# Block-sparse attention with a gated MLP on one core: batch 0's PSUM evictions, a dealing table and two early copies

## The chip, the core and the metric

The kernel runs on one core of a Trainium2 chip. Five engines have queues of their own: PE (TensorE, the matmuls), DVE (VectorE), ACT (ScalarE), POOL (GpSimd) and SP (SyncE, which issues most transfers here). The metric is the device time of one launch in microseconds, the median over runs. Lower is better.

## The reference

Attention over 4 batches, 8 heads, 768 positions and 64 dimensions, with a block mask (blocks of 32: neighbours, first and last blocks, and three sampled blocks per row); its output, heads side by side, goes into a gated MLP that mixes along the sequence.

```python
scores = scale * np.matmul(q, k.transpose(0, 1, 3, 2))
scores = np.where(mask, scores, -1000000000.0)
scores = scores - np.max(scores, axis=-1, keepdims=True)
attn = np.exp(scores)
attn = attn / (np.sum(attn, axis=-1, keepdims=True) + 1e-09)
x = np.matmul(attn, v)            # to (batch, seq, heads*dim)
...
h = np.maximum(x @ w_in, 0.0)
u, v = (h[..., :d_ff // 2].copy(), h[..., d_ff // 2:].copy())
mu = np.mean(v, axis=-1, keepdims=True)
var = np.mean((v - mu) ** 2, axis=-1, keepdims=True)
v_n = (v - mu) / np.sqrt(var + 1e-06)
v_s = np.einsum('ts,bsd->btd', w_spatial, v_n) + b_spatial[None, :, None]
gated = u * v_s
return (gated @ w_out).astype(np.float32)
```

## The kernel before

**Pairs and slots.** Two heads of a batch make a pair: 16 pairs, 4 to a batch. The order of all work is written out by hand as a list of slots (the loop at L837). Slots 0 to 35 do the four pairs of batch 0 in thirds of the queries, as its inputs arrive. From slot 36 on, a head takes six slots, one for each 128 keys, and a pair twelve; pair p starts at slot 36 + 12(p - 4) (`slot_of`, L805). Slots 36 to 83 hold batch 1's scores, 84 to 131 batch 2's, 132 to 179 batch 3's.

**What a slot does.** In order: two score matmuls into a PSUM tile "sc" (L455) and one exponential of it on ACT (L459); six matmuls of probabilities times values (L506) of the head seven slots back; whatever `when` put into the slot; some steps of the queue of gMLP matmuls (`run_queue`, L707); and what was put off to its end. PSUM has two "sc" tiles, so a slot's scores need the exponential of two slots before to be over, two "av" tiles for the values' product, and two banks "moeA" and "moeB" that the gMLP products (and some transposes) take in turn. A head's last slot divides by the sums on DVE: a reciprocal (L470) and a multiplication (L471), "the scaling" below.

**The gMLP of a batch** runs beside the attention of the next one, as products of 128 tokens by 512, each a list of steps of one matmul of 128x512 (`product`, L573; all have line L580). v0 to v5 and u0 to u5 (four steps each) are the two halves of x times `w_in`; s0 to s5 (six steps) are the spatial mix of the normalized v; o0 to o5 (four steps) the product with `w_out`. The last step of a product calls `done`, which records its eviction from the bank:
- v: maximum with 0 on DVE (L610; ACT in the last batch), and its statistics; POOL makes the reciprocal deviation; the norm (L634) comes some steps later on DVE, and all that are left just before s0 (L695);
- u: maximum with 0, on DVE for u0 to u3 of batch 0 (L640), on ACT for the others (L642). The helper `ts` records at L186;
- s: plus bias, times u, on DVE (L648); after every second one a transposing DMA from SP (L658) makes the operand of o;
- o: a copy into a result tile `osb`, on ACT for even and on DVE for odd numbers (L675; the copies record at L221 and L218), followed by its DMA to memory from SP (L677).

**How the steps are dealt.** `STEPS` (L771) fixes the number of steps for slots 20 to 41. At slot 42 the last 16 input steps of batch 0, its 36 spatial and 24 output steps, 76 in all, are dealt over 50 slots by a running credit (L712 to L719), which gives 1 or 2 a slot. At slots 92 and 140 the gMLP of batches 1 and 2 starts: 108 steps over 48 slots.

**The score operands.** q and k of pairs 4 to 15 are loaded, cast on POOL (L137), transposed by a DMA from SP (`tr_dma`, L411, tile `tt`, 20 slots before the pair's start), and copied to `kq` by DVE, one head at a time: `split(p, 0)` five slots before the pair starts (L814) and `split(p, 1)` three before (L815), 64x1536 each, recorded at L218. `tt` has two buffers. Pair 9 starts at slot 96 and pair 13 at slot 144.

**In-order queues.** Each engine does its instructions in the order in which they were recorded, slot by slot: an instruction that waits holds up all that were recorded behind it on its engine.

Of the kernel before, what the change touches and what calls it, by code (L numbers as in the profile page):

```python
# [26 lines left out]
def kernel(  # L27
# [37 lines left out]
    TW = TC * 128  # L65
    S0 = NT * NG * 3
    FILL, FILL2, FILL3 = 24, 4, 4
    U_DVE = (0, 1, 2, 3)

    const = ctx.enter_context(tc.tile_pool(name="const", bufs=1))  # L70
    work = ctx.enter_context(tc.tile_pool(name="work", bufs=1))
# [112 lines left out]
    def ts(out, in0, s1, o0, s2=None, o1=None):  # L184
        kw = {} if o1 is None else {"op1": o1}
        nc.vector.tensor_scalar(out=out, in0=in0, scalar1=s1, scalar2=s2, op0=o0, **kw)  # L186
# [334 lines left out]
    def xtr_pe(p, xn, c0, n, ps=None):  # L521
        if ps is None:
            ps = bank()
        for c in range(n):
            tr(ps, c, pair_of(xn, c))
        dve_copy(xt_tile(p)[:, c0 * 128:(c0 + n) * 128], ps[:, 0:n * 128])
# [46 lines left out]
    def product(n, lhs, rhs, last, done, w=512):  # L573
        ref = {}
        out = []
        for i in range(n):
            def run(i=i):
                if i == 0:
                    ref["ps"] = moe_ps(last)
                nc.tensor.matmul(out=ref["ps"][:, 0:w], lhsT=lhs(i), rhs=rhs(i),  # L580
                                 start=(i == 0), stop=(i == n - 1))
                if i == n - 1:
                    done(ref["ps"][:, 0:w])
            out.append(run)
        return out
# [4 lines left out]
    class Moe:  # L590
# [45 lines left out]

        def u_product(self, tcc):
            def done(ps):
                if self.b == 0 and tcc in U_DVE:
                    ts(self.un[:, tcc, :], ps, 0.0, ALU.max)  # L640
                else:
                    nc.scalar.activation(out=self.un[:, tcc, :], in_=ps, func=AF.Relu)  # L642
            return product(NDM, lambda g: self.xt(g, tcc), lambda g: w_in_t[:, g, 0:DH],
                           self.last, done)
# [19 lines left out]
        def o_product(self, tcc):  # L664
            steps = []
            osb = {}
            parts = 2 if self.last and tcc == NCH - 1 else 1
            w = DM // parts
            for i in range(parts):
                cs = slice(i * w, (i + 1) * w)  # L670

                def done(ps, i=i, cs=cs):
                    if i == 0:
                        osb["t"] = work.tile([128, DM], FP32, tag="osb", bufs=6, name="osb")
                    on_act = (tcc + i) % 2 == 0  # L675
                    (act_copy if on_act else dve_copy)(osb["t"][:, cs], ps)
                    (nc.scalar if i or (self.last and tcc == 0) else nc.sync).dma_start(  # L677
                        out=out[self.b].rearrange("(p c) d -> c p d", c=NCH)[tcc][:, cs],
                        in_=osb["t"][:, cs])
                steps += product(NDH, lambda d: self.gt[:, tcc, d, :],  # L680
                                 lambda d, cs=cs: w_out_t[:, d, cs], self.last, done, w)
            return steps
# [20 lines left out]
    def deal(steps, slots):  # L703
        queue.extend(steps)
        pace["slots"], pace["credit"] = slots, 0.0

    def run_queue(n=None):  # L707
        if n is not None:
            for _ in range(n):
                queue.popleft()()  # L710
            return
        if not queue or pace["slots"] <= 0:  # L712
            return
        pace["credit"] += (len(queue) - pace["credit"]) / pace["slots"]
        pace["slots"] -= 1
        n = int(pace["credit"] + 0.5)
        for _ in range(min(n, len(queue))):
            queue.popleft()()
            pace["credit"] -= 1  # L719
# [5 lines left out]
    def when(slot, *fns):  # L725
        at.setdefault(slot, []).extend(fns)

    def c(f, *a, **kw):
        return lambda: f(*a, **kw)
# [29 lines left out]
    def close_first():  # L759
        first["steps"].popleft()()  # L760
        if moe_tags[0] not in held:
# [7 lines left out]
    when(20, close_first)  # L769
    when(29, lambda: deal(moe[0].in_steps("v2 v3 u2 u3", TC), 14))  # L770
    STEPS = {20: 1, 21: 2, 22: 1, 23: 1, 24: 2, 25: 1, 26: 1, 27: 2, 28: 1, 29: 1, 30: 1, 31: 1, 32: 2, 33: 1, 34: 1, 35: 1, 36: 1, 37: 0, 38: 1, 39: 2, 40: 2, 41: 2}  # L771
    when(42, lambda: deal(moe[0].in_steps("v4 v5 u4 u5", TC) + moe[0].rest_steps(),
                          S0 + 8 + 48 - 42))
    for b in (1, 2):
# [30 lines left out]
    def slot_of(p):  # L805
        return S0 + 12 * (p - NG)

    for p in range(NG, NP):
        g = slot_of(p)
        when({4: 13, 5: 22, 6: 31}.get(p, g - 34), c(load, p, "k"), c(load, p, "q"), c(load, p, "v"))  # L810
        when({4: 18, 5: 26, 6: 38}.get(p, g - 25),
             c(cast, p, "k", PL), c(cast, p, "q", PL), c(cast, p, "v", PL))
        when({4: 20, 5: 30}.get(p, g - 20), c(tr_dma, p))
        when(g - 5, c(split, p, 0))  # L814
        when(g - 3, c(split, p, 1))  # L815
        if p == NP - 1:
            when(g + 20, last_x)
        elif p % NG == NG - 1:
            when(g + 20, lambda p=p: xtr_pe(p, xn_ref.pop(("p", p)), 0, NCH))
        else:  # L820
            when(g + 20, c(xtr_dma, p))
# [15 lines left out]
    for s in range(NS + LAG + 2):  # L837
# [11 lines left out]
        for f in early:  # L849
            f()  # L850
        run_queue(STEPS.get(s))
        for f in late.get(s, []):
# [34 lines left out]
```

## Time and profile before

| | |
|---|---|
| Median of 3 runs | 212.64 us (212.44 to 212.85) |
| The profiled execution | 212.95 us |
| Its span, first to last instruction | 211.1 us (211.06) |
| Granted TensorE clock | 0.999 |
| PE busy | 205.2 us, 2141 matmuls |
| ACT busy | 169.8 us, 225 instructions |
| DVE busy | 129.3 us, 290 instructions |
| POOL busy | 69.8 us |
| Exponential of a slot from 36 on (L459) | 144, median 0.811 us |
| u evictions of batch 0 on DVE, 128x512 from PSUM (L186) | 4, 0.692 us each |
| u evictions on ACT out of moeA and moeB (L642) | 14, median 0.592 us |
| o evictions on ACT out of moeA and moeB (L221) | 9, median 0.592 us |
| Copy of a score operand to `kq` from `tt` (L218) | 24, median 0.555 us |
| Transposing DMA into `tt`, issue to landing | median 6.6 us, 3.8 to 8.5 |

A matmul's busy time in the profile includes its way through the array, and matmuls overlap, so "97% busy" does not say that PE never stands still. The starts say it: matmuls that wait for nothing start at a fixed distance from one another. An exponential starts some 0.69 to 0.71 us after the one before where it waits for nothing, though its own time is 0.81, since instructions of ACT and DVE overlap by their last part.

### The profile page before, as it was taken

To read this page: it belongs to the slowest core of one execution; us is meant where nothing else is said; L and a number is where in the kernel's file an instruction comes from. 1 tells how busy PE (TensorE), PEld (TensorE's weight loads), DVE (VectorE), ACT (ScalarE), POOL (GpSimd) and SP (SyncE) were. 2 spreads that over 40 slices of the span, in tenths; PEclk is the share of its full clock that TensorE was granted. 3 is DMA by queue.
4 is the path that set the end of the run, shared out by engine and by line. 5 is a ranking of instruction groups with operands and counts; after the bars stand their busy time and mean duration, and the time that the engine had idled before them with its cause. 6 is when DMAs were issued, how large, how long until landed. Compare 5 with 4: busy or idle time off the path is not lost.

```text
span 211.1 us, 5272 instructions
## 1 busy us (share of the span) xinstructions
PE 205.2 (97%) x2141; PEld 128.7 (61%) x2141; DVE 129.3 (61%) x290; ACT 169.8 (80%) x225; POOL 69.8 (33%) x108
## 2 busy tenths in 40 slices
PE   8998999999999999999999999999999999999993
PEld 6687878765666665665565566565565566544441
DVE  6798584687844534385888445287685433567542
ACT  5798999998999999979999788979989878266021
POOL 6583959756574224042533031040120000003000
PEclk9999999999999999999999999999999999999999
DMA  5999899999999999999991399695100423520276
GB/s 161 347 340 296 248 338 295 302 189 293 254 368 237 271 188 314 219 290 370 131 282 36 60 245 224 205 274 160 37 3 5 80 54 77 208 103 0 40 163 246
DMA packets 64295, 41.97 MB, mean 199 GB/s; under 512 B 45184, under 2 KB 59024, under 8 KB 64272
## 3 DMA queue, kind: packets, MB, share of 16 engines
q1 hardware_dynamic: 63696, 41.06, 76.0%
q10 hardware_dynamic: 576, 0.59, 0.8%
q8 instruction: 16, 0.26, 0.5%
q14 instruction: 7, 0.06, 0.1%
HBM read 24.38 MB, written 6.29 MB: 145 GB/s over the span
## 4 chain that ended last, share of the span: by engine, by line
PE 81%; DMA 10%; ACT 2%; DVE 1%; POOL 1%; SPq 1%; issue 1%; ACTq 0%
PE ps_moe L580 30%; PE ps L455 22%; PE ps_av L506 12%; PE ps_t L580 8%; DMA tt<-nat 4%; DMA w_f<-in_moe_w_in_dram 4%; PE ps_sc L580 4%; DMA ws_f<-in_moe_w_spatial_dram 3%; PE ps L442 2%; PE wps L180 1%; ACT a_all L459 1%; DVE kq L218 1%; PE ps_av L488 1%; POOL w_in_t L234 1%; PE ps L289 1%
## 5 line engine op out<-in xcount | busy, mean ns | idle before, releaser
L459 ACT ACTIVATE a_all<-ps 128x768 bf16<-128x768 f32 x144 | 113.8, 813 | 14.0 <-PE ps L455 7.0
L455 PE MATMUL ps<-kq 88*128 88x384 bf16 x288 | 70.4, 325 | 0.2
L506 PEld LDWEIGHTS <-a_all 128*128 128x128 bf16 x864 | 45.2, 97 | 20.0
L506 PE MATMUL ps_av<-vv,a_all 128*128 128x65 bf16 x864 | 49.8, 193 | 0.0
L455 PEld LDWEIGHTS <-kq 88*128 88x128 bf16 x288 | 28.0, 97 | 31.2 <-issue 1.1
L580 PE MATMUL ps_moe<-w_in_t,xt 128*128 128x512 bf16 x144 | 43.8, 378 | 0.2 <-POOL w_in_t L234 0.2
L447 ACT ACTIVATE a_all<-ps 128x1024 bf16<-128x1024 f32 x36 | 34.9, 1025 | 3.1 <-PE ps L442 2.5
L580 PE MATMUL ps_moe<-vn,w_spt 128*128 128x512 bf16 x108 | 32.7, 378 | 0.0
L137 POOL CAST nat<-st_k 128x768 bf16<-128x768 f32 (+2 forms) x17 | 13.6, 803 | 44.3 <-DMA st_k<-in_k_dram 43.6
L442 PE MATMUL ps<-kq 88*128 88x256 bf16 (+1 forms) x140 | 23.0, 287 | 0.2 <-ACT a_all L447 0.2
L470 DVE RECIPROCAL rc<-ps_av 128x6 f32<-128x6 f32 (+1 forms) x36 | 6.6, 184 | 26.7 <-PE ps_av L506 25.9
L648 DVE SCALAR_TENSOR_TENSOR un<-ps_moe,b_col,un 128x512 bf16<-128x512 f32 x18 | 13.5, 750 | 15.3 <-PE ps_moe L580 14.7
L617 POOL TENSOR_SCALAR std<-mv 128x3 f32<-128x3 f32 (+1 forms) x9 | 2.2, 240 | 59.9 <-DVE mv L614 43.9
L580 PE MATMUL ps_moe<-w_out_t,gt 128*128 128x512 bf16 x72 | 21.5, 378 | 0.0
L580 PEld LDWEIGHTS <-xt 128*128 128x128 bf16 x192 | 15.5, 98 | 7.3 <-DVE xt L218 0.2
L471 DVE TENSOR_TENSOR xn<-ps_av,rc 128x384 bf16<-128x384 f32 (+1 forms) x36 | 18.5, 513 | 1.2
L613 DVE BATCH_NORM_STATS2 stats<-vn 128x6 f32<-128x512 bf16 x24 | 16.5, 687 | 1.4 <-ACT vn L608 0.9
L137 POOL CAST nat<-st_q 128x768 bf16<-128x768 f32 (+2 forms) x21 | 14.5, 695 | 7.8 <-DMA st_q<-in_q_dram 7.6
L137 POOL CAST vv<-st_v 128x768 bf16<-128x768 f32 x16 | 13.6, 848 | 7.9 <-DMA st_v<-in_v_dram 7.7
L442 PEld LDWEIGHTS <-kq 88*128 88x128 bf16 x140 | 13.0, 100 | 4.5 <-issue 0.8
L218 DVE COPY kq<-tt 64x1536 bf16<-64x1536 bf16 x24 | 14.3, 595 | 2.3 <-DMA tt<-nat 2.1
L580 PEld LDWEIGHTS <-w_spt 128*128 128x128 bf16 x144 | 11.4, 98 | 5.2
(81 smaller groups left out, 205.8 us busy)
## 6 DMA issues: line engine op xcount, KB each, us to landing
st_v<-in_v_dram SPq DMA_DIRECT2D x16, 384.0 KB, 6.0
st_k<-in_k_dram SPq DMA_DIRECT2D x15, 384.0 KB, 4.0
out_dram<-osb SPq DMA_DIRECT2D x22, 256.0 KB, 3.5
st_q<-in_q_dram SPq DMA_DIRECT2D x12, 384.0 KB, 5.4
ws_f<-in_moe_w_spatial_dram SPq DMA_DIRECT2D x6, 384.0 KB, 9.0
w_f<-in_moe_w_in_dram SPq DMA_DIRECT2D x8, 256.0 KB, 7.9
w_f<-in_moe_w_out_dram SPq DMA_DIRECT2D x4, 256.0 KB, 4.0
st_q<-in_q_dram SPq DMA_DIRECT2D x6, 128.0 KB, 5.4
```

The source lines that it names most:

```text
L137: eng.tensor_copy(out=dst, in_=src)
L218: nc.vector.tensor_copy(out=o, in_=i)
L442: nc.tensor.matmul(out=ps[:, at:at + n * TW], lhsT=kq[:, h, ci * 128:(ci + 1) * 128], rhs=kq[:, h, qcols(t0, n)], start=True, stop=True)
L447: nc.scalar.activation(out=out, in_=ps, func=AF.Exp, scale=0.125)
L455: nc.tensor.matmul(out=ps[:, hf * 512:hf * 512 + HALF], lhsT=kq[:, j % H, ci * 128:(ci + 1) * 128], rhs=kq[:, j % H, S + hf * HALF:S + (hf ...
L459: nc.scalar.activation(out=a_ref["h", j][:, ci, :].rearrange("p (b c) -> p b c", b=2), in_=ps.rearrange("p (b c) -> p b c", b=2)[:, :, 0:H ...
L470: nc.vector.reciprocal(out=rc[:, 0:n], in_=ps[:, :, D:VA])
L471: nc.vector.tensor_tensor(out=out, in0=ps[:, :, 0:D], in1=rc[:, 0:n].to_broadcast([128, n, D]), op=ALU.mult)
L506: nc.tensor.matmul(out=av_ref[j][:, qc, 0:VA], lhsT=a_ref["h", j][:, ci, qc * 128:(qc + 1) * 128], rhs=vv[p % NVV][:, h, ci, 0:VA], start= ...
L580: nc.tensor.matmul(out=ref["ps"][:, 0:w], lhsT=lhs(i), rhs=rhs(i), start=(i == 0), stop=(i == n - 1))
L613: nc.vector.bn_stats(out=stats, in_=self.vn[:, tcc, :])
L648: nc.vector.scalar_tensor_tensor(out=self.un[:, tcc, :], in0=ps, scalar=b_col[:, tcc:tcc + 1], in1=self.un[:, tcc, :], op0=ALU.add, op1=AL ...
```

## The change

Three things. (1) In batch 0, u4 and u5 and then o0, o2 and o4 are evicted by DVE too, so all of its u and o products are. (2) `STEPS` gets entries for slots 42 to 91, so the credit rule no longer decides there; the steps themselves and their order stay. (3) For pairs 9 and 13 the first of the two copies to `kq` is recorded seven slots before the pair's start (slots 89 and 137) instead of five (91 and 139). The numbers of instructions on PE, POOL and SP and their order there stay, but for the place of three gMLP matmuls among PE's; DVE gets five instructions more and ACT five fewer.

```diff
@@ -65,7 +65,6 @@
     FILL, FILL2, FILL3 = 24, 4, 4
-    U_DVE = (0, 1, 2, 3)
@@ -636,7 +635,7 @@
         def u_product(self, tcc):
             def done(ps):
-                if self.b == 0 and tcc in U_DVE:
+                if self.b == 0:
                     ts(self.un[:, tcc, :], ps, 0.0, ALU.max)
                 else:
                     nc.scalar.activation(out=self.un[:, tcc, :], in_=ps, func=AF.Relu)
@@ -672,7 +671,7 @@
-                    on_act = (tcc + i) % 2 == 0
+                    on_act = (tcc + i) % 2 == 0 and (self.last or self.b > 0)
                     (act_copy if on_act else dve_copy)(osb["t"][:, cs], ps)
@@ -769,6 +768,8 @@
     STEPS = {20: 1, 21: 2, 22: 1, 23: 1, 24: 2, 25: 1, 26: 1, 27: 2, 28: 1, 29: 1, 30: 1, 31: 1, 32: 2, 33: 1, 34: 1, 35: 1, 36: 1, 37: 0, 38: 1, 39: 2, 40: 2, 41: 2}
+    STEPS.update({s: 2 if (s % 2 == 0) == (s < 67) else 1 for s in range(42, 92)})
+    STEPS.update({43: 2, 46: 1})
     when(42, lambda: deal(moe[0].in_steps("v4 v5 u4 u5", TC) + moe[0].rest_steps(),
                           S0 + 8 + 48 - 42))
@@ -811,7 +812,7 @@
-        when(g - 5, c(split, p, 0))
+        when(g - (7 if p in (9, 13) else 5), c(split, p, 0))
         when(g - 3, c(split, p, 1))
```

## The prediction

> **What bounds the kernel now.** I read the page first: the busy shares and the chain that ended last.
>
> ```profile
> PE 205.2 (97%) x2141; PEld 128.7 (61%) x2141; DVE 129.3 (61%) x290; ACT 169.8 (80%) x225; POOL 69.8 (33%) x108
> ...
> PE 81%; DMA 10%; ACT 2%; DVE 1%; POOL 1%; SPq 1%; issue 1%; ACTq 0%
> ```
>
> TensorE is the bound, and the other engines hold 2% and 1% of the chain. A change that leaves TensorE's instructions as they are, as this one does, can only win back the moments in which TensorE stands still. Second I read the chain in order of time from 47 to 58 us (start, duration, what) to price a slot.
>
> ```profile
> 48.05 0.31 issue
> 48.37 0.82 ACT a_all L459
> 49.19 0.04 issue
> 49.23 0.48 PE ps L455 x2
> ...
> 51.99 0.33 PE ps L455 x2
> ...
> 52.72 0.33 PE ps L455 x2
> ...
> 53.66 0.33 PE ps L455 x2
> ```
>
> A slot begins with its two score matmuls (L455). From 51.99 to 52.72 is a slot with one gMLP matmul, 0.73; from 52.72 to 53.66 one with two, 0.94. So a slot is 0.51 for scores and attention (0.33 + 0.18) and 0.215 for each gMLP matmul. Laying this grid over the score starts from slot 36 (42.65 us) to the last slot leaves five holes after 43 us: 0.27 in slot 43 (48.23 to 49.23 with one gMLP matmul, 1.00 against 0.73), 0.18 in slot 51, 0.24 in slot 80, and 0.15 and 0.10 where batches 1 and 2 begin (slots 92 and 140). All else is on the grid within 0.01. The change can reach about 0.9 us at most.
>
> Third I looked for what made each hole. Slot 43: the first lines above. The exponential of slot 42 starts 0.31 after the last one ended, for no cause that the profile shows ("issue"), and the score bank that slot 44 needs comes free so much later. Slot 51, in TensorE's timeline:
>
> ```profile
> 55.17 0.49 PE L455 MATMUL ps<-kq 88*128 88x384 bf16 x2
> ...
> 56.08 0.48 PE L455 MATMUL ps<-kq 88*128 88x384 bf16 x2
> ...
> 56.80 0.38 PE L580 MATMUL ps_moe<-vn,w_spt 128*128 128x512 bf16 x1
> ```
>
> 0.91 for a slot of 0.73. ScalarE evicts u4 at 54.73, ahead of slot 50's exponential (55.21 to 56.03), which holds the score bank that slot 52 needs. Slot 80 is the same with o0, in ScalarE's timeline:
>
> ```profile
> 79.28 0.59 ACT L221 ACTIVATE osb<-ps_moe 128x512 f32<-128x512 f32 x1
> ```
>
> The scores at 80.62 wait for the exponential behind it. The other three evictions (u5 57.31, o2 83.52, o4 88.53) cost TensorE nothing: the slots around them are on the grid. Slot 92's hole is VectorE's:
>
> ```profile
> 89.65 0.54 DVE L218 COPY kq<-tt 64x1536 bf16<-64x1536 bf16 x1
> 90.16 0.69 DVE L218 COPY osb<-ps_moe 128x512 f32<-128x512 f32 x1
> ```
>
> v0 of batch 1 needs o5's bank and starts at 90.90, that is 0.05 after this eviction ends; six transposes from 90.42 at 0.055 would have let it start at 90.75.
>
> **The table.** The old rule dealt 76 gMLP matmuls over slots 42 to 91 as 2,1,2,1,2,1,1,2,1,2... Written out, the table gives the same count in every slot but two: slot 43 gets 2 instead of 1, slot 46 gets 1 instead of 2. So v4's last matmul and the next two come a slot earlier; 73 of 76 stay. Slot 43 then has 0.94 of work in the 1.00 that it lasts anyway, and slot 46 shrinks from 0.94 to 0.73: **-0.215**. v4's eviction does not move: VectorE runs back to back there (norm 50.26, eviction 51.09), and v5's first matmul waits for u3's eviction, over at 48.36. If the pause at 48.05 does not come, slot 43 grows by what slot 46 shrinks: 0.
>
> **The u evictions.** Two ScalarE instructions of 0.59 to 0.62 go; slot 51 returns to 0.73: **-0.18**. Two VectorE instructions come; the rows for the same shape (u0 to u3) are 0.692 each. They stand behind the attention scaling of 55.40 and ahead of the two norms:
>
> ```profile
> 55.40 0.56 DVE L471 TENSOR_TENSOR xn<-ps_av,rc 128x384 bf16<-128x384 f32 x1
> 56.45 1.24 DVE L186 TENSOR_SCALAR vn<-vn,mv,rstd 128x512 bf16<-128x512 bf16 x2 [0.49 <-POOL rstd L619]
> ```
>
> From 49.46 to 55.96 VectorE has no idle time, and its start there is set by GpSimd (rstd, 48.70 + 0.73), not by TensorE: this run of work does not move with the gain. After such a scaling the next instruction starts 0.475 later (89.18 to 89.65), so u4's eviction runs from 55.88 to 56.57. Its bank is the one that the first spatial product s0 takes. s0 started at 56.805; by the two gains it would be ready at 56.805 - 0.215 - 0.18 = 56.41, and can start at 56.57 + 0.05 = 56.62: **+0.21**, a new wait. u5's eviction follows at 56.6 (its last matmul ends then) to 57.3, the norms to 58.2 or, stretched as the second is now, 58.5; s0's fifth and sixth matmuls need them at 59.0 and 59.7, the attention scaling behind them moves from 58.45 to at most 58.5, and its bank is not asked for before slot 61. Nothing for these.
> By the row the move costs 0.10 more per eviction than on ScalarE (0.692 against 0.59). The Trainium skill speaks against it too: "Perfetto Trace Analysis", section Optimizing Scalar/DVE Operations, gives a fixed cost of about 125 ns for VectorE on PSUM and about 51 ns for ScalarE. By that the move would cost 0.074, and the new wait would come out at an estimated 0.18; the trace agrees in sign and is the dearer.
>
> **The o evictions.** Three of 0.59 leave ScalarE; slot 80 returns to 0.73: **-0.24**. Three VectorE copies of 0.692 (rows of o1, o3, o5) come. o0 goes in at 79.40 behind a scaling and pushes the two score-operand copies to 81.2, wanted at slot 84 (83.2). o2 fills idle time at 83.4; the reciprocal behind it moves from 83.94 to 84.1. o4 ends at 88.9, where the reciprocal waited until 88.95. The banks are asked for 1.9 to 2.2 us after these ends (slots 81, 87, 92). SP, which sends the results in order, is busy with a transpose until 83.5 when o0 is ready and sends o2 at 87.0 and o4 at 93.2 as now. Nothing but the gain.
>
> **The two splits.** Each is one VectorE copy of 0.54, no DMA; its transfer is issued where it was. Pair 9's goes from behind the scaling of 89.18 to before o4's eviction, where VectorE idles from 86.57. o5's eviction then waits for its matmul alone (ends 90.07): 90.10 instead of 90.16, **-0.05**. Pair 13's leaves 137.73, but the eviction behind it (138.40) already starts 0.04 after its matmul (137.99 + 0.38): 0. The copies' sources landed at 85.5 and 129.1 by the semaphore's events, before the new places (86.6, 135.8).
>
> **Sum.** -0.215 - 0.18 + 0.21 - 0.24 - 0.05 = -0.475. From slot 92 on only slot 140 and the last output have holes (0.10 each), both of TensorE's own timing, so the gain should reach the end. The profiled execution took 212.95 (span 211.06 and 1.89 around it), 0.31 above the median of the three runs, 212.64. It would come to 212.48; the median to 212.64 - 0.475 = **212.17**.
>
> **Rivals.**
> *The pause is chance.* The gap at 48.05 is the only one of its kind on ScalarE in the trace, and the profiled execution is the slowest of the four times, by 0.31 against the median. Then the table gives nothing, and s0 would have started at 56.54 before; after, still 56.62: +0.08. With -0.24 and -0.05 the gain is 0.21: 212.43. Against it: every wait of that exponential had long been met, so it may be part of the program's own stream, which is unchanged there.
> *No new wait.* In VectorE's full stretch one norm took 0.91 (50.26) where its neighbour took 0.41, and a copy 1.02 (52.73) where others take 0.55, each while GpSimd cast (50.20, 52.51). If the loads that start those casts land 0.3 earlier or later, the stretch ends 0.5 or 0.95 sooner, and s0 does not wait: -0.685, 211.95. The skill's page "SBUF — State Buffer", Who interferes with whom, says that a VectorE instruction in a two-port mode and GpSimd lock each other out for a whole instruction; these rows agree.
> *The early split blocks VectorE: slower.* In its new place pair 9's copy stands ahead of o4's eviction, the last scaling of batch 0's queue, o5's eviction and v0. Issued at 80.29, its source took 5.2 us; such transposes took 3.8 to 8.5. At 8.5 it lands at 88.8; then copy to 89.35, o4 to 90.0, reciprocal and scaling to 90.7, o5 to 91.4, v0 at 91.45 against 90.43: +1.02, 0.55 slower than before, 213.19. It begins to cost at a landing of 87.3, and has eaten the gain at 88.2. For it: its queue is loaded there; against it: 1.8 us to spare in this trace.
> *It does not do what it says.* The table moves three matmuls, so half of the sum hangs on slots 51 and 80; if other executions have holes elsewhere the time stays: 212.6.
>
> **How the numbers follow.** A difference under 0.2% (0.43 us) can't be told from none. Forecast 0.50, of which 0.33 lies beyond 0.43 and 0.17 within, since 0.475 is so near; pause by chance 0.20 (within); no new wait 0.17 (faster); blocked split 0.08 (slower); no effect 0.05 (within). Faster 0.50, same 0.42, slower 0.08. The range takes the cases from 211.95 to 212.6 with the runs' own spread (0.2 each way): 211.8 to 212.8, leaving out the slower case and the edges.
>
> **What would show it.** Right: score starts 0.73 apart across slots 46, 51 and 80; s0's first matmul 0.05 after a VectorE un eviction that ends near 56.6; v0 of batch 1 at 90.4; batch 1's slots on the same grid. Wrong: a hole of 0.1 or more in slots 76 to 92 behind VectorE, a copy that waits for its transpose near 87 to 89, or a grid that is itself slower.

## The result, and the profile after

| | before | changed |
|---|---|---|
| Median of 15 runs each, side by side | 212.42 us (211.98 to 213.35) | 211.59 us (210.38 to 212.13) |
| Changed to before, 95% interval | | 0.9957 (0.994 to 0.9974) |
| Profiled execution | 212.95 us | 211.57 us |
| Its span | 211.06 us | 209.80 us |
| Start to the scores of slot 37 | 43.60 | 42.76 |
| Scores of slot 37 to scores of slot 179 | 133.94 | 133.33 |
| From there to the last matmul's end | 30.06 | 30.04 |
| Last matmul's end to the span's end | 3.46 | 3.67 |

The changed kernel is faster, by 0.4%, and by the first comparison it lies just below the range forecast. The lower rows part the two spans (43.60 + 133.94 + 30.06 + 3.46 = 211.06) and already say that the 1.26 us between them are of three kinds: 0.84 lies before slot 37, where no instruction was changed; 0.61 lies in the slots that the change reaches; and 0.21 is given back at the very end.

The page of the profile after: the shares of the engines, and the chain that ended last.

```profile
PE 203.2 (97%) x2141; PEld 127.8 (61%) x2141; DVE 134.2 (64%) x295; ACT 167.8 (80%) x220; POOL 69.3 (33%) x108
...
PE 86%; DVE 6%; DMA 4%; ACT 2%; POOL 1%; issue 0%; ACTq 0%; SPq 0%
```

The five instructions have gone from ACT (225 to 220) to DVE (290 to 295), and PE is still the bound. The chain runs through DVE and DMA (6% and 4%) only in the first 42.3 us, and through PE alone from there to the last output. Line numbers of the changed kernel are one lower than those of before: scores L454, exponential L458, gMLP L579.

TensorE's timeline of the changed kernel, in the slots where the prediction put its first two terms and its new wait (start, duration, what):

```profile
47.39 0.49 PE L454 MATMUL ps<-kq 88*128 88x384 bf16 x2
...
47.90 0.59 PE L579 MATMUL ps_moe<-w_in_t,xt 128*128 128x512 bf16 x2
48.38 0.48 PE L454 MATMUL ps<-kq 88*128 88x384 bf16 x2
...
54.11 0.49 PE L454 MATMUL ps<-kq 88*128 88x384 bf16 x2
...
54.84 0.49 PE L454 MATMUL ps<-kq 88*128 88x384 bf16 x2
...
55.56 0.38 PE L579 MATMUL ps_moe<-vn,w_spt 128*128 128x512 bf16 x1
55.78 0.49 PE L454 MATMUL ps<-kq 88*128 88x384 bf16 x2
```

Slot 43 (47.39 to 48.38) holds two gMLP matmuls now, and with the pause in it still lasts 0.99. Slot 51, from 54.11 to 54.84, is 0.73, not the 0.91 of before. Slot 52 (54.84 to 55.78) holds one more u5 matmul and s0's first, and is 0.94, exactly two gMLP matmuls: the wait of 0.21 that the prediction put in front of s0 is not there. VectorE's timeline says why:

```profile
47.74 0.41 DVE L185 TENSOR_SCALAR vn<-vn,mv,rstd 128x512 bf16<-128x512 bf16 x1 [0.22 <-POOL rstd L618]
48.07 0.54 DVE L217 COPY kq<-tt 64x1536 bf16<-64x1536 bf16 x1
48.53 0.91 DVE L185 TENSOR_SCALAR vn<-vn,mv,rstd 128x512 bf16<-128x512 bf16 x1
...
53.67 0.56 DVE L470 TENSOR_TENSOR xn<-ps_av,rc 128x384 bf16<-128x384 f32 x1
54.15 0.68 DVE L185 TENSOR_SCALAR un<-ps_moe 128x512 bf16<-128x512 f32 x1
...
86.95 0.55 DVE L217 COPY kq<-tt 64x1536 bf16<-64x1536 bf16 x1 [1.86 <-DMA tt<-nat]
87.43 0.68 DVE L217 COPY osb<-ps_moe 128x512 f32<-128x512 f32 x1
...
88.72 0.68 DVE L217 COPY osb<-ps_moe 128x512 f32<-128x512 f32 x1
```

u4's eviction (54.15 to 54.83) stands right behind the scaling, 0.48 after its start, as forecast. But the whole stretch began at 47.74, only 0.35 after the scores of slot 43 (47.39); before, it began at 49.46, 1.23 after them (48.23). VectorE is 0.88 earlier against TensorE, and s0's bank is free 0.73 before s0 comes. The stretched norm (0.91) is still there, so the stretch did not become shorter; it was begun earlier. The lines of before on which this rests, of GpSimd and VectorE:

```profile
43.96 0.83 POOL L137 CAST vv<-st_v 128x768 bf16<-128x768 f32 x1 [1.84 <-DMA st_v<-in_v_dram]
45.23 3.07 POOL L552 CAST ws_b<-ws_f 128x768 bf16<-128x768 f32 x2 [0.44 <-DMA w_spt<-ws_b]
...
48.70 0.73 POOL L619 TENSOR_TENSOR rstd<-std,mhalf 128x2 f32<-128x2 f32 x1
49.46 0.41 DVE L186 TENSOR_SCALAR vn<-vn,mv,rstd 128x512 bf16<-128x512 bf16 x1 [1.10 <-POOL rstd L619]
```

The last three lines of the changed kernel's VectorE timeline, from 86.95, are pair 9's early copy and the evictions of o4 and o5. The copy waited for its transpose (idle 1.86, released by the DMA), o4's eviction followed at 87.43 and o5's at 88.72, behind VectorE's own work and not behind its matmul. Slot 92's hole is 0.18 against 0.15 before: what the slower rival described did begin, and cost 0.03.

### The profile page after: what moved, and what is told of

Read it like the earlier page. It is cut to its first block, busy times and chain, and to the rows that moved or that the text cites. A ratio compares the mean times of both kernels' runs of the same rounds, so it can differ in the third digit from the quotient of the medians.

```text
span 209.8 us, 5271 instructions
## 1 busy us (share of the span) xinstructions
PE 203.2 (97%) x2141; PEld 127.8 (61%) x2141; DVE 134.2 (64%) x295; ACT 167.8 (80%) x220; POOL 69.3 (33%) x108
## 4 chain that ended last, share of the span: by engine, by line
PE 86%; DVE 6%; DMA 4%; ACT 2%; POOL 1%; issue 0%; ACTq 0%; SPq 0%
PE ps_moe L579 32%; PE ps L454 22%; PE ps_av L505 13%; PE ps_t L579 8%; DMA w_f<-in_moe_w_in_dram 4%; PE ps_sc L579 4%; PE ps L441 3%; DVE kq L217 2%; PE ps_av L487 2%; ACT a_all L446 1%; DVE vn L185 1%; PE wps L179 1%; PE ps L288 1%; DVE stats L612 1%; DVE xn L470 1%; POOL w_in_t L233 1%
## 5 line engine op out<-in xcount | busy, mean ns | idle before, releaser
L458 ACT ACTIVATE a_all<-ps 128x768 bf16<-128x768 f32 x144 | 114.1, 811 | 15.1 <-PE ps L454 7.4
L454 PE MATMUL ps<-kq 88*128 88x384 bf16 x288 | 70.4, 325 | 0.0
L454 PEld LDWEIGHTS <-kq 88*128 88x128 bf16 x288 | 28.0, 97 | 30.6 <-issue 0.2
L579 PE MATMUL ps_moe<-w_in_t,xt 128*128 128x512 bf16 x144 | 43.8, 378 | 0.6 <-POOL w_in_t L233 0.6
L579 PE MATMUL ps_moe<-vn,w_spt 128*128 128x512 bf16 x108 | 32.7, 377 | 0.0
L441 PE MATMUL ps<-kq 88*128 88x256 bf16 (+1 forms) x140 | 21.7, 275 | 1.0 <-DVE kq L217 0.5
L579 PE MATMUL ps_moe<-w_out_t,gt 128*128 128x512 bf16 x72 | 21.5, 378 | 0.0
L579 PEld LDWEIGHTS <-xt 128*128 128x128 bf16 x192 | 15.5, 98 | 7.3 <-DVE xt L217 0.2
L217 DVE COPY kq<-tt 64x1536 bf16<-64x1536 bf16 x24 | 15.6, 650 | 2.5 <-DMA tt<-nat 2.2
L579 PEld LDWEIGHTS <-w_spt 128*128 128x128 bf16 x144 | 11.4, 98 | 5.2
```

What stands on the lines that cost most here:

```text
L217: nc.vector.tensor_copy(out=o, in_=i)
L441: nc.tensor.matmul(out=ps[:, at:at + n * TW], lhsT=kq[:, h, ci * 128:(ci + 1) * 128], rhs=kq[:, h, qcols(t0, n)], start=True, stop=True)
L454: nc.tensor.matmul(out=ps[:, hf * 512:hf * 512 + HALF], lhsT=kq[:, j % H, ci * 128:(ci + 1) * 128], rhs=kq[:, j % H, S + hf * HALF:S + (hf ...
L458: nc.scalar.activation(out=a_ref["h", j][:, ci, :].rearrange("p (b c) -> p b c", b=2), in_=ps.rearrange("p (b c) -> p b c", b=2)[:, :, 0:H ...
```

## The experiments

All holes below are by the grid of the prediction (0.51 and 0.215 for each gMLP matmul, and 0.33 for the six transposes of slots 92 and 140), in slots 43 to 178; slots 37 to 42 hold other matmuls and are alike within 0.02 in all profiles. "37 to 179" is the time between the scores of these two slots.

| Kernel | 37 to 179, us | holes over 0.1, by slot | first norm behind slot 43's scores | last matmul's end to span's end |
|---|---|---|---|---|
| before | 133.94 | 43: 0.27, 51: 0.18, 80: 0.24, 92: 0.15, 140: 0.10 | 1.23 | 3.46 |
| changed | 133.33 | 92: 0.18, 140: 0.10 | 0.35 | 3.67 |
| e1_table | 134.11 | 51: 0.18, 80: 0.24, 92: 0.16, 140: 0.49 | 0.61 | 3.47 |
| e2_u | 133.80 | 43: 0.27, 80: 0.24, 92: 0.16, 140: 0.14 | 0.05 | 3.49 |
| e3_o | 133.71 | 43: 0.28, 51: 0.18, 92: 0.16, 140: 0.10 | 0.38 | 3.68 |
| e4_split | 133.94 | 43: 0.27, 51: 0.18, 80: 0.24, 92: 0.16, 140: 0.10 | 1.30 | 3.53 |
| a2_again | 133.32 | 92: 0.16, 140: 0.10 | 0.05 | 3.72 |
| a3_again | 133.31 | 92: 0.15, 140: 0.10 | 0.05 | 3.68 |
| a_no_split | 133.32 | 92: 0.16, 140: 0.10 | 0.05 | 3.64 |
| a_before2 | 133.94 | 43: 0.27, 51: 0.18, 80: 0.24, 92: 0.16, 140: 0.10 | 0.05 | 3.45 |
| b_act4 | 133.69 | 51: 0.18, 80: 0.24, 92: 0.16, 140: 0.10 | 0.05 | 3.51 |
| a_late_deal | 132.86 | none | 0.05 | 3.65 |
| a_late_act4 | 132.80 | none | 0.40 | 3.66 |
| a_dve_late2 | 137.04 | 52: 2.09, 54 to 56: 1.64 in all, 92: 0.16, 140: 0.10 | 0.72 | 3.64 |

### One part of the change at a time

**e1_table**: the kernel before with the table alone.

```diff
+    STEPS.update({s: 2 if (s % 2 == 0) == (s < 67) else 1 for s in range(42, 92)})
+    STEPS.update({43: 2, 46: 1})
```

> The kernel before with the table alone. Theory A (each part fills its own hole in TensorE's grid of slots; what lies before slot 36 differs from execution to execution and has nothing to do with the change): slot 43 keeps its length near 1.0 us with two gMLP matmuls in it, slot 46 shrinks from 0.94 to 0.73, the holes of slots 51 and 80 stay, so slots 37 to 178 get 0.2 shorter; time lower by 0.2 (0.1%). Theory B (the parts only pay together, or the gain lies in slots 0 to 35, through where instructions lie in their streams): less than 0.05 between slots 37 and 178, or a slot 36 that starts 0.5 or more before 42.6. If the pause of 0.31 on ScalarE in slot 42 is chance, it is missing here and nothing is gained.

Slot 43 went from a hole of 0.27 to 0.05 with the same pause in it: the second matmul lies where TensorE stood. Against before, 37 to 179 is 0.18 longer, since a hole of 0.39 more opened in slot 140, far behind the table's slots; without it the gain is 0.21. Time 212.26 (12 runs) against 212.61 (35 runs), ratio 0.999 (0.9961 to 1.0019). The new hole is the one that the split of pair 13 is about. VectorE's timeline of this kernel there:

```profile
137.72 1.16 DVE L218 COPY kq<-tt 64x1536 bf16<-64x1536 bf16 x1
138.80 0.67 DVE L218 COPY osb<-ps_moe 128x512 f32<-128x512 f32 x1
```

and TensorE's:

```profile
138.70 0.50 PE L289 MATMUL ps<-ident,xn 128*128 128x128 bf16 x6
139.53 0.59 PE L580 MATMUL ps_moe<-w_in_t,xt 128*128 128x512 bf16 x2 [0.33 <-DVE osb L218]
```

In the old place the copy can take 1.16 and not 0.54: here GpSimd casts beside it (137.64 to 138.47), while in the profile of before that cast was over at 137.69 and the copy began at 137.73. o5's eviction then ends at 139.47, and v0 of batch 2 waits for it until 139.53.

**e2_u**: the u evictions alone.

```diff
-                if self.b == 0 and tcc in U_DVE:
+                if self.b == 0:
```

> The kernel before with u4 and u5 of batch 0 evicted by VectorE, nothing else. Theory A: slot 51's hole (0.18) is gone, s0's first matmul waits for u4's eviction only if VectorE's full stretch (the norm behind the first rstd) starts 1.0 us or more after slot 43's scores, as in the profile of before (1.23); then s0 would start without the table's gain at about the same time as the eviction ends, so 0.1 to 0.18 gained between slots 37 and 178. Theory B: nothing there, gain in slots 0 to 35 or none.

The hole of slot 51 (0.18) went, and nothing came in slot 52. TensorE's timeline shows slots 51 and 52 at 0.72 and 0.95:

```profile
55.09 0.49 PE L455 MATMUL ps<-kq 88*128 88x384 bf16 x2
...
55.81 0.49 PE L455 MATMUL ps<-kq 88*128 88x384 bf16 x2
...
56.54 0.38 PE L580 MATMUL ps_moe<-vn,w_spt 128*128 128x512 bf16 x1
56.76 0.49 PE L455 MATMUL ps<-kq 88*128 88x384 bf16 x2
```

VectorE evicted u4 at 54.45, and s0 came at 56.54. The start of VectorE's stretch was 0.05 behind slot 43's scores. Time 211.93, ratio 0.9986 (0.9956 to 1.0016).

**e3_o**: the o evictions alone.

```diff
-                    on_act = (tcc + i) % 2 == 0
+                    on_act = (tcc + i) % 2 == 0 and (self.last or self.b > 0)
```

> The kernel before with o0, o2 and o4 of batch 0 evicted by VectorE, nothing else. Theory A: slot 80 goes from 0.97 to 0.73, slots 43 and 51 keep their holes, slot 92's hole stays at 0.15 or grows by up to 0.1 since o4's eviction and the copy now both stand ahead of o5's: 0.15 to 0.25 gained between slots 37 and 178, time lower by 0.1%. Theory B: nothing there.

The hole of slot 80 (0.24) went; the slot is 0.73 long:

```profile
78.12 0.49 PE L455 MATMUL ps<-kq 88*128 88x384 bf16 x2
...
78.85 0.49 PE L455 MATMUL ps<-kq 88*128 88x384 bf16 x2
```

The end grew by 0.2, to 3.68. Time 212.07, ratio 0.9994 (0.9966 to 1.0021).

**e4_split**: the two early copies alone.

```diff
-        when(g - 5, c(split, p, 0))
+        when(g - (7 if p in (9, 13) else 5), c(split, p, 0))
```

> The kernel before with the first copies of pairs 9 and 13 two slots sooner, nothing else. Theory A: slot 92's hole shrinks by 0.05 at most where pair 9's transpose has landed by 86.5, and grows where it lands later than 87.3; slot 140 unchanged at 0.10; time the same within 0.1%. Theory B: a gain of 0.2 or more from this part.

Nothing moved: 37 to 179 in 133.94, slot 92's hole 0.157 (0.154 before). Time 212.67, ratio 1.0007 (0.9981 to 1.0033). VectorE's timeline of this kernel ahead of slot 92:

```profile
88.21 0.55 DVE L218 COPY kq<-tt 64x1536 bf16<-64x1536 bf16 x1 [1.58 <-DMA tt<-nat]
89.00 0.20 DVE L470 RECIPROCAL rc<-ps_av 128x6 f32<-128x6 f32 x1 [0.24 <-PE ps_av L506]
...
90.21 0.69 DVE L218 COPY osb<-ps_moe 128x512 f32<-128x512 f32 x1 [0.42 <-PE ps_moe L580]
```

With the copy out of the way, o5's eviction still starts only when its matmul is over ("<-PE ps_moe"), at the same place on TensorE's grid. So TensorE itself set it before too, and the copy ahead of it was not what it waited for. The early copy again waited 1.58 for its transpose, here without cost.

The parts add up: 0.21 + 0.18 + 0.24 = 0.63, less 0.03 in slot 92, gives 0.60, and the changed kernel gained 0.61. None of the four times can be told from the kernel before: every interval holds 1. What each part does is read from the grid.

### Is the new wait real, and what decides it?

**a_before2**: the kernel before, profiled once more, with no edit.

> The kernel before, unchanged, profiled once more. My theory: its holes in slots 43, 51 and 80 come again within 0.02 (0.27, 0.18, 0.24), its time from slot 37 to 179 is 133.94 within 0.05; VectorE's first norm starts anywhere from 0.05 to 1.3 behind slot 43's scores, and the start of slot 36 lies anywhere from 41.1 to 42.9. The rival (the late start of VectorE, 1.23, is a property of the kernel before): 1.2 to 1.3 again.

VectorE's timeline of this run:

```profile
46.97 0.69 DVE L186 TENSOR_SCALAR un<-ps_moe 128x512 bf16<-128x512 f32 x1 [0.47 <-PE ps_moe L580]
47.58 0.53 DVE L186 TENSOR_SCALAR vn<-vn,mv,rstd 128x512 bf16<-128x512 bf16 x1
48.03 0.54 DVE L218 COPY kq<-tt 64x1536 bf16<-64x1536 bf16 x1
48.50 0.40 DVE L186 TENSOR_SCALAR vn<-vn,mv,rstd 128x512 bf16<-128x512 bf16 x1
49.45 0.69 DVE L186 TENSOR_SCALAR vn<-ps_moe 128x512 bf16<-128x512 f32 x1 [0.55 <-PE ps_moe L580]
```

The same kernel as in the prediction, and none of what the prediction read there: the first norm follows u3's eviction at once, 0.05 behind slot 43's scores (47.53), the second takes 0.40, and VectorE then idles 0.55 for TensorE. The holes are the same within 0.01 and so is 37 to 179, 133.94 (one run, 212.73 us). So the holes are a property of the kernel, and the late start of VectorE was one of that execution. GpSimd's timeline of this run says what differed:

```profile
42.29 3.09 POOL L552 CAST ws_b<-ws_f 128x768 bf16<-128x768 f32 x2 [1.81 <-DMA w_spt<-ws_b]
...
45.77 0.73 POOL L619 TENSOR_TENSOR rstd<-std,mhalf 128x2 f32<-128x2 f32 x1
```

In the profile of before GpSimd stood 1.84 for a load of v (`st_v`), until 43.96, and its long cast of `w_spatial` started 3.00 ahead of slot 43's scores. Here it could cast that load at 39.65, the long cast started 5.24 ahead of them, and the reciprocal deviation (`rstd`) was there long before the norm asked for it.

**a_dve_late2**: the changed kernel with VectorE made late by six memsets. They write a tile that nothing reads.

```diff
+    late_t = const.tile([128, 256], FP32, name="late_t")
...
+    when(49, lambda: [nc.vector.memset(late_t, 0.0) for _ in range(6)])
```

> The changed kernel with six memsets of a 128x256 tile (read by nobody) recorded on VectorE in slot 49, inside the stretch in which it has no idle time. My theory (s0 waits by how late VectorE's stretch runs: wait = start of the first norm behind slot 43's scores, plus the time D that the six take, minus 1.04): the hole that the prediction expected appears at s0 in slot 52, about D minus 0.7 to 1.0 long (0.3 or more if one memset takes 0.2 or more), and s0's first matmul starts 0.05 after the end of u4's eviction; if D stays under 0.7 there is none. The rival (s0's start hangs on TensorE's own queue, so VectorE's lateness never shows there): s0 on its grid and no hole in slot 52, whatever D is.

VectorE's timeline of this kernel:

```profile
47.31 0.41 DVE L186 TENSOR_SCALAR vn<-vn,mv,rstd 128x512 bf16<-128x512 bf16 x1 [0.59 <-POOL rstd L619]
...
54.03 2.23 DVE L766 MEMSET late_t<- 128x256 f32 x6
56.17 1.22 DVE L186 TENSOR_SCALAR un<-ps_moe 128x512 bf16<-128x512 f32 x2
```

and TensorE's:

```profile
54.55 0.38 PE L580 MATMUL ps_moe<-w_in_t,xt 128*128 128x512 bf16 x1
56.85 0.38 PE L580 MATMUL ps_moe<-vn,w_spt 128*128 128x512 bf16 x1 [1.93 <-DVE un L186]
57.07 0.49 PE L455 MATMUL ps<-kq 88*128 88x384 bf16 x2
```

s0 now waits for the eviction, by name ("<-DVE un"), and the hole in slot 52 is 2.09. From the first norm to u4's eviction it is 8.86 here (47.31 to 56.17), against the 6.42 that the prediction worked out (49.46 to 55.88), 2.44 more; the stretch began 0.72 behind slot 43's scores; 0.72 + 2.44 - 1.04 = 2.12. The mechanism of the term is right, and so is its threshold for a stretch of 6.42: s0 waits once VectorE begins more than about 1.04 behind. A longer or shorter stretch moves it. In the seven profiles that evict u4 on VectorE without memsets, the eviction was over 0.69 to 1.41 before s0 came, so the threshold lay at 0.74 to 1.41; 0.74 is a_late_deal, which began only 0.05 behind but had a copy of 1.18 and a norm of 1.05. A start later than 1.04 came in 2 of 14 profiles (before 1.23, e4_split 1.30), both of kernels that evict u4 on ScalarE, where nothing waits for it.

The second cost was not expected. The view of stretches of this kernel (from and to, length, busy time of PE, PEld, DVE, ACT and POOL, granted TensorE clock, DMA share, GB/s):

```profile
54.00:56.00 2.00, 0.93 (x10) 0.47 (x9) 1.40 (x7) 1.38 (x2) 2.00 (x3) 1.00 1.20 213
...
59.00:60.00 1.00, 1.00 (x8) 0.53 (x7) 0.94 (x2) 0.19 (x1) 0.89 (x2) 0.50 1.06 389
60.00:61.00 1.00, 1.00 (x9) 0.54 (x7) 0.00 (x0) 0.81 (x1) 0.97 (x2) 0.50 1.05 369
...
62.00:64.00 2.00, 2.00 (x22) 1.24 (x21) 1.67 (x2) 1.63 (x3) 1.56 (x3) 1.00 1.18 319
```

After TensorE had stood for 1.93, its granted clock was 0.50 from 58.3 to 61.7, and slots 54 to 56 took 1.64 more. A small wait costs its own length; this one cost 2.09 + 1.64, and the time was 214.46 (one run), the slowest here. The Trainium skill, "TensorE: Matmul & The Clock Gate", Part 1: The HAM clock gate, describes two clocks, full and half, and a window of 3413 ns; the half clock and the 3.4 us that it lasted agree. The same page of the Trainium skill, in its section Why this matters for your kernels, warns of idle stretches over some 3 us; here, in one run, one of 1.93 was enough. The next longest in any profile, 1.14 us in e4_split (from 16.58), left the clock full. The recorded stretches of full clock in this trace last 54.61 and 150.19 us, 16 and 44 times the 3.413 of the half clock, so the clock seems to change on a fixed beat; the beat that ended with the drop, 54.93 to 58.34, holds the whole wait.

### The surplus of the first comparison

**a2_again**, **a3_again**: the changed kernel with no edit, on two other occasions.

> The changed kernel once more, unaltered. Theory A (the change fills TensorE's holes in slots 43, 51 and 80; what lies before slot 36 is chance): slots 37 to 179 take 133.3 again, and if VectorE's first norm comes x us after slot 43's scores, s0 waits x - 1.04 where that is positive (x was 0.35 in its first profile, 0.05 to 1.30 in the others); slot 36 starts anywhere between 41.1 and 42.9, as in the kernels with one part each. Theory B (part of the 0.8 us comes from slots 0 to 35, through the change): slot 36 starts near 41.7 again. Time 0.55 to 1.2 below the kernel before.

> The changed kernel once more beside the kernel before. My theory (0.61 on the grid, 0.17 given back at the end, 0.07 from slot 140 on the mean): 0.5 below the kernel before, ratio 0.9975 with an interval that holds 0.997 to 0.998; slots 37 to 179 in 133.33, no hole in slot 52. The rival (the first comparison's 0.83 is the true size): ratio 0.996.

211.77 against 212.42, ratio 0.9971 (0.9955 to 0.9986); and 211.85 against 212.13, ratio 0.9992 (0.9967 to 1.0016). The second interval holds the 0.997 to 0.998 of my theory, though its centre is above them and it holds 1 as well; the rival's 0.996 lies outside it. The time from slot 37 to 179 agreed with the first profile to 0.02 both times, and s0 did not wait. Slot 36 began at 42.20 and 41.92, after 41.67 in the first profile of the changed kernel; in the two of the kernel before it began at 42.65 and 42.08. The two ranges overlap, so these five profiles do not show that the change shortens slots 0 to 35, nor do they exclude a few tenths: the pooled difference below is 0.14 more than the 0.43 of the grid and the end. Over the three comparisons the mean is 211.80 (39 runs) against 212.37 (61 runs), 0.57 less; drawing from these runs again and again gives 0.34 to 0.80 as 95% interval. The 0.83 of the first medians was a draw from the far side.

**a_no_split**: the changed kernel with both copies in their old place (`when(g - 5, ...)`).

> The changed kernel with both first copies back at five slots before their pairs. My theory (the early copies gain nothing on the grid; pair 13's only spares a long copy now and then): slots 37 to 179 in 133.33 as in the changed kernel, or up to 0.4 more where GpSimd's cast meets the copy ahead of slot 140, a hole of 0.15 to 0.16 in slot 92; the median within 0.1 of the changed kernel's beside it. The rival (what the changed kernel gained beyond the 0.61 of its table and evictions less 0.17 at the end comes from the splits): the median 0.25 or more above the changed kernel's, and the hole of slot 140 0.3 or more in the profile.

37 to 179 in 133.32, as with the splits, slot 140's hole 0.10. The median, 212.11, is 0.26 above that of the changed kernel beside it (211.85), as the rival said; but the other half of what it said, 0.3 or more in slot 140, is not in the profile, and both kernels' runs spread over more than 2 us (211.07 to 213.61, and 211.22 to 213.48). The means differ by 0.10 (212.23 and 212.13). Undecided by the times; by the grid the splits give nothing in this profile.

### ScalarE's pause

**b_act4**: the kernel before with four tiny copies (they change nothing that is read) on ScalarE in slots 26 to 32.

```diff
+    for s in (26, 28, 30, 32):
+        when(s, lambda: nc.scalar.activation(out=tiny, in_=tiny, func=AF.Copy))
```

> The kernel before with four tiny ScalarE copies (128x1, one each in slots 26, 28, 30 and 32). The pause of 0.31 us on ScalarE ahead of slot 42's exponential came in all six profiles. If it belongs to a place in ScalarE's stream of instructions (the 64th or so), it now comes four instructions earlier, ahead of the exponential of slot 38; if it belongs to something that happens beside it (a transfer, GpSimd, the start of a new probabilities tile), it stays ahead of slot 42's.

ScalarE's timeline of the changed kernel (the pause is there: idle 0.32 behind its own last instruction):

```profile
45.52 1.68 ACT L458 ACTIVATE a_all<-ps 128x768 bf16<-128x768 f32 x2
47.52 3.13 ACT L458 ACTIVATE a_all<-ps 128x768 bf16<-128x768 f32 x4 [0.32 <-ACT a_all L458]
```

and of b_act4:

```profile
43.33 7.11 ACT L459 ACTIVATE a_all<-ps 128x768 bf16<-128x768 f32 x9
```

Nine exponentials without a break, and no hole in slot 43: 37 to 179 is 0.25 shorter than before, by adding work (one run, 211.8 us). The pause came in all 12 profiles without these copies, in the same place, though GpSimd's work beside it lay up to 2.3 us earlier or later, and in neither of the two with them, though the same exponential starts a new head there too. So it goes with ScalarE's own stream of instructions, and four more of them ahead of it did away with it there. I had expected to see it in another slot. Whether it has moved under running work or is gone was not shown, nor what it is.

### Versions that go further

**a_late_deal**: the changed kernel with the products of batches 1 and 2 dealt one slot later, over 47 slots, so that v0 does not ask for o5's bank in slot 92 and 140.

```diff
-        when(s0, c(moe_begin, b),
-             lambda b=b: deal(moe[b].in_steps(SEQ, 3) + moe[b].rest_steps(), 48))
+        when(s0, c(moe_begin, b))
+        when(s0 + 1, lambda b=b: deal(moe[b].in_steps(SEQ, 3) + moe[b].rest_steps(), 47))
```

> The changed kernel with the gMLP matmuls of batches 1 and 2 dealt from one slot later on (slots 93 and 141, 108 over 47 slots instead of 48). Theory A: v0 no longer stands between the transposes and the eviction of o5, so the holes of slots 92 (0.15 to 0.18) and 140 (0.10, 0.49 in one profile) are gone and no new one comes: slots 37 to 179 take 133.0 to 133.1, time 0.28 below the changed kernel. Rival: the steps crowd together and the exponentials or VectorE become the bound of a slot, so that holes of the same sum turn up after slot 93.

TensorE's timeline of this kernel around slot 92:

```profile
89.10 0.50 PE L288 MATMUL ps<-ident,xn 128*128 128x128 bf16 x6
89.43 0.49 PE L454 MATMUL ps<-kq 88*128 88x384 bf16 x2
...
89.94 0.59 PE L579 MATMUL ps_moe<-w_in_t,xt 128*128 128x512 bf16 x2
```

The scores follow the transposes 0.33 later (six at 0.055), with no gMLP matmul and no wait between. Both holes are gone. 37 to 179 is 0.46 shorter than in a2_again, of which 0.22 (one matmul moved behind slot 179) comes back: 30.26 from slot 179 to the last matmul, not 30.04. Time 211.55 (12 runs) against 211.77 of a2_again beside it, which the runs alone do not part (their means are 0.08 apart); ratio to before 0.9979 (0.9955 to 1.0002).

**a_late_act4**: that, and the four copies of b_act4.

> The changed kernel with the dealing of batches 1 and 2 one slot later over 47 slots, and four tiny ScalarE copies in slots 26 to 32. My theory (the pause of ScalarE belongs to a place in its stream and the copies shift it under an exponential): no hole in slot 43 (0.05 before), none in slots 92 and 140, slots 37 to 179 in 132.80 (132.86 without the copies), time as without them within 0.1, some 211.5, below the changed kernel. The rival (with fewer ScalarE evictions the boundary falls elsewhere): a hole of up to 0.3 in another slot, 133.1.

Not one hole over 0.1 is left from slot 43 to slot 178, and 37 to 179 is 132.80, the shortest of all. Time 211.32 against 212.25, ratio 0.9964 (0.993 to 0.9998). By the grid it is 0.29 ahead of the changed kernel (132.80 + 0.22 against 133.31); the two did not run side by side, and their medians (211.32; 211.59 to 211.85) are closer than their runs spread.

## Why the prediction was off, step by step

**The table, -0.215: right.** e1_table shows it (slot 43: 0.27 to 0.05). The rival that the pause is chance fell: 12 of 12. The old dealing that the prediction writes out is misread: in the trace of before it is 2,1 without a break up to slot 65, then 2 and 2, then 1,2. Nothing hangs on that, since slots 43 and 46 are the two that differ.

**The u evictions, -0.18: right.** e2_u shows it.

**The new wait of s0, +0.21: the step that failed.** The prediction took VectorE's start at 49.46 as fixed by GpSimd and so "this run of work does not move with the gain". GpSimd did set it in that execution, but its casts wait for loads: the cast of the same load began at 43.96 in that profile and at 39.65 in a_before2, which runs the same code. What made the load later was not followed further. a_before2 has the kernel before with VectorE in step with TensorE, the seven profiles of kernels with the u evictions on VectorE and no memsets have no wait, and a_dve_late2 has the wait when VectorE is late. The term should have been a cost of 0.2 to 0.3 with a small chance. The rival "No new wait" had the right outcome and not quite the right cause: it looked for shorter norms and copies inside the stretch, but in the changed kernel's first profile they were as long as before (0.91, and 1.01 for the copy), and the earlier start alone made the difference.

**The o evictions, -0.24: right** (e3_o), with a cost that was not in the sum: the end of the kernel is 3.64 to 3.72 in all eight profiles that have this part and 3.45 to 3.53 in the six that do not, +0.18 on the mean (3.67 and 3.49). Nearly all of it lies in the program's closing line, DRAIN and EVENT_SEMAPHORE instructions on every engine: from SyncE's first DRAIN there to the span's end it is 0.94 or 0.95 in the eight and 0.77 in the six. It is paid behind the last matmul, where the prediction said that the gain would arrive untouched.

**The splits, -0.05 and 0: the first was wrong.** o5's eviction was held by its own matmul (e4_split). The price that the slower rival named began to show: the copy waited for its transpose in the changed kernel, in e4_split and in a_late_act4 (idle 1.12, up to 86.57), at a cost of 0.03 at most. For pair 13 the old place carries a risk that the prediction did not see: 0.39 in e1_table, 0.04 in e2_u, nothing in five others, so 0.06 on the mean of these seven profiles. No run shows the early place paying it.

**The sum and the range.** By the grid and the end, -0.61 + 0.18 = -0.43, close to the -0.475 forecast, but that is luck: the wait that did not come and the end that was not seen nearly cancel. The pooled -0.57 (-0.80 to -0.34) agrees with both. What took the first median out of the range was its base and its width: 212.64 was the median of three runs, while 15 runs give 212.42, and "the runs' own spread" of 0.2 came from these three, while single runs of the kernel before went from 210.74 to 213.99. From 212.42 the same sum gives 211.95. That the first comparison was 0.4 lower still is not explained by a mechanism that any run shows.

## What to carry to other kernels

Before a term is built on where one engine stands against another, ask what started that stretch: if it goes back to a load, it is a draw, and a second profile of the same kernel shows it for the price of one run. Holes that come again to 0.01 in every profile are worth planning on; a start that differs by 1.2 is not. And an engine that is off the path has room up to a threshold: work out that threshold (here 1.04, and 0.74 to 1.41 with the stretches of other executions) and give the chance of passing it, not the wait of the one execution.

## What the runs showed of the hardware beyond that

- A pause of 0.32 to 0.33 on ScalarE came ahead of the same exponential in 12 of 12 profiles; with four more instructions ahead of it, it did not come (2 of 2 profiles), which won 0.25.
- In one run 1.93 us without a matmul were followed by a granted clock of 0.50 for about 3.4 us, from 1.5 us after the matmuls had begun again; 1.14 us in another run were not.
- Three evictions moved between engines near 80 us changed the end of the program, from 3.5 to 3.7 behind the last matmul, and nearly all of it in the program's closing line (0.94 and not 0.77). SyncE's stream has one semaphore instruction fewer in those kernels (71 and not 72); that this is the cause is only argued.
- Slots 0 to 35, the same code in all but for the four tiny copies of two kernels, brought slot 36 to its start anywhere from 41.0 to 42.9: over half of the difference between the first two spans (0.84 of 1.26) is this.
- Transposes of one kind, issued at one place, landed late enough in some executions to hold up a copy that had 1.1 us to spare in the profile of before.
